# The last rows of a dense matrix in column halves, and its sum in two PSUM banks

## Chip, cores and metric

The kernel runs on one core of one Trainium2 chip. The metric is the device time of one execution in microseconds; lower is better.

## What is computed

A decode step for two sequences (B = 2, one token each, D = 448): the token's row is layer-normed, and the output is the row itself plus attention over the last 4,096 positions of a key and value cache plus a dense block with a Mish activation.

```python
xn = layernorm(x)                                   # 2 x 448
q = xn @ wq                                         # 448 x 4096: 16 heads of 256
s = q . k_cache[:, :, Sk - 4096:]  * 256 ** -0.5    # 8 kv heads, each for two query heads
o = softmax(s) . v_cache[:, :, Sk - 4096:]
A = o.reshape(2, 4096) @ wo                         # 4096 x 448
h = xn @ w1 + b1                                    # 448 x 1792
Bm = (h * tanh(softplus(h))) @ w2                   # 1792 x 448: the second dense matrix
out = x + A + Bm                                    # 2 x 448, bfloat16
```

All inputs are bfloat16. Keys and values of the window are 2 x 8 x 4,096 x 256 each, so 67 MB of the 78 MB that the kernel reads.

## The kernel before

The work goes in eight steps u = 0 to 7 of two kv heads each (`U = 8`, `KU = 2`). For each step the keys come in two loads of 4 MB (`load_k`), the values in two (`load_v`), and one load has the rows of `wo` that belong to its heads (`load_wo`). All of these loads, and those of `w1` and `w2`, are issued from SyncE's queue (SP) in the order in which the program names them. A load waits until its buffer is free: the big ones share a ring of three buffers (`ring`), which the keys, the values, `wq`, `w1` and `w2` take in turn. The schedule is written out by hand (`tc.manual_schedule()`): each engine runs its instructions in program order.

In a step VectorE transposes the keys in 32 x 32 blocks (`turns`, L271), TensorE makes the scores (`scores`, L347 and L358) into a PSUM tile `sc`, for which there are two buffers, ScalarE takes the exponential (L366), and VectorE turns the result into the layout that `values` needs (L369, L338 to L340). `values` (L404) multiplies it with the value rows, `weigh` makes the softmax denominators, `gather` and `finish` put the heads' outputs together and divide.

Steps 0 to 6 add their outputs times `wo` into the PSUM tile `early`. The last step does not: its value load is cut into pieces, so that the work behind the last value bytes is short, and its output goes through `mix` into a second sum, `acc`. That sum is laid out in four column groups of 112 (`G = 4`, `DG = 112`): group g lies on partitions 32g and 32g + 1, so the four groups of one product are four matmuls on four column blocks of TensorE. `carry` (L238, L240) copies `early` into `acc`'s groups, `add_rows` (L251) adds a product to all four.

The second dense matrix `w2` has 1,792 rows of 448. It is split in two halves k = 0 and 1 of 896 rows, and in each half partition p holds seven consecutive rows (`NI = 7`), 6,272 bytes that lie together in HBM. It is loaded last, behind the last values, in four parts (L556): (k, first row, last row + 1) of each partition are

```python
w2_parts = ((0, 0, NI), (1, 0, 4), (1, 4, 6), (1, 6, NI))
```

so 784, 448, 224 and 112 KB. `dense_out` takes the parts in the same order and makes one product for each row index i, four matmuls through `add_rows`. The activations `act_bf` that it multiplies are ready since the first step. At the end four copies move the groups of `acc` into the bfloat16 row `res`, groups 0 and 2 on VectorE (L621) and groups 1 and 3 on ScalarE (L623), and one store writes it (L624):

```python
for g in range(G):
    dst = res[:, g * DG : (g + 1) * DG]
    src = acc[32 * g : 32 * g + Bsz, :]
    if g % 2 == 0:
        nc.vector.tensor_copy(out=dst, in_=src)
    else:
        nc.scalar.copy(out=dst, in_=src)
nc.sync.dma_start(out=out.flatten_outer_dims(), in_=res[:])
```

The end of the program, in order: the loads of the last values, of the last `wo` rows and of the four parts of `w2`; `carry`; the last `values`, `weigh`, `gather`, `values_fixed` and `finish`; `mix`; the four `dense_out`; the copies and the store.

Of the kernel before, what the change touches and what calls it, by code (L numbers as in the profile page):

```python
# [12 lines left out]
FP32 = mybir.dt.float32  # L13
# [4 lines left out]
def kernel(  # L18
# [13 lines left out]
    nc = tc.nc  # L32
    P = 128
    G = 4
# [4 lines left out]
    Bsz, Sq, D = A_x.shape  # L39
# [22 lines left out]
    NI = F2 // P  # L62
    DG = D // G
# [14 lines left out]
    ps_sc = ctx.enter_context(tc.tile_pool(name="ps_sc", bufs=2, space=PSUM))  # L78
# [3 lines left out]
    ps_a = ctx.enter_context(tc.tile_pool(name="ps_a", bufs=1, space=PSUM))  # L82
# [7 lines left out]
    def ring(name):  # L90
        return kv_pool.tile([P, RK * KE], BF16, tag="kv", name=name)
# [18 lines left out]
    def load_wo(u):  # L110
# [22 lines left out]
        out=wq[:, 0 : NS * HW], in_=A_wq.flatten().rearrange("(p e) -> p e", p=P)  # L133
# [14 lines left out]
    for k in range(KU):  # L148
        nc.gpsimd.tensor_copy(
            out=hot[:, k, :, :, :, k],  # L150
            in_=ident[:].rearrange("p (q y) -> p y q", y=4).unsqueeze(2)
# [11 lines left out]
        out=rstd[:], in_=mv[:, 1:2], func=ACT.Sqrt, bias=eps_t[:], scale=1.0  # L163
# [4 lines left out]
        out=xn_bf[:],  # L168
# [8 lines left out]
        out=parm[:], in_=ident[:].rearrange("p (a o) -> p o a", o=2), axis=AXIS.X, op=ALU.add  # L177
# [3 lines left out]
        out=jm[:],  # L181
        in_=ident[:].rearrange("p (a j h) -> p j a h", j=J, h=rep),
# [4 lines left out]
        out=jm[:], in0=jm[:], scalar1=-1.0, scalar2=29952.0, op0=ALU.add, op1=ALU.mult  # L187
# [3 lines left out]
        out=mneg[:], in_=jm[:].unsqueeze(1).to_broadcast([P, TH * 8, J])  # L191
    )
    sel = consts.tile([P, 2, NQ], FP32)
    for x in range(2):
        for w in range(4):
            at = 32 * w + (2 * (w % 2) + x) * NQ
            src = ident[:, at : at + NQ]
            if w == 0:
                nc.vector.tensor_copy(out=sel[:, x, :], in_=src)
            else:  # L200
                nc.vector.tensor_tensor(
                    out=sel[:, x, :], in0=sel[:, x, :], in1=src, op=ALU.add
# [16 lines left out]
    for odd in range(2):  # L219
        for half in range(2):  # L220
            o = (half + odd) % 2
            nc.vector.tensor_scalar(
                out=xs[:, odd::2, half * Bsz : (half + 1) * Bsz],
# [7 lines left out]
    nc.tensor.matmul(  # L231
        early[:], lhsT=ident[0:Bsz, 0:Bsz], rhs=x_bf[:], start=True, stop=False
    )
    acc = ps_a.tile([P, DG], FP32)

    def carry():
        e_sb = small.tile([P, 2 * Dh], FP32, tag="vs", name="e_sb", bufs=1)[0:Bsz, 0:D]
        nc.scalar.copy(out=e_sb, in_=early[:])  # L238
        for g in range(G):
            nc.tensor.matmul(  # L240
                acc[32 * g : 32 * g + Bsz, :],
                lhsT=id2[:],
                rhs=e_sb[:, g * DG : (g + 1) * DG],
                start=True,
                stop=False,
                skip_group_check=True,
            )

    def add_rows(lhsT, rows, stop=False):
        for g in range(G):  # L250
            nc.tensor.matmul(  # L251
                acc[32 * g : 32 * g + Bsz, :],
                lhsT=lhsT,
                rhs=rows[:, g * DG : (g + 1) * DG],
                start=False,
                stop=stop,
                skip_group_check=True,
            )
# [20 lines left out]
    for n in range(2):  # L279
        for e in range(2):  # L280
# [3 lines left out]
                out=sp[:],  # L284
                in_=ident[:, o : o + 63 : 2].unsqueeze(1).to_broadcast([P, G, 32]),
# [91 lines left out]
    state = {}  # L377
# [113 lines left out]
    def mix(u):  # L491
        oT, w = state.pop(("oT", u)), wo_t.pop(u)
        for k2 in range(KU):
            for h in range(rep):
                for c in range(2):
                    add_rows(oT[:, c, k2 * rep + h, :], w[:, k2, h, c * D : (c + 1) * D])

    act_bf = consts.tile([P, NI, 2, Bsz], BF16)
# [46 lines left out]
        nc.vector.tensor_tensor(out=act_bf[:], in0=h_sb[:], in1=t_sb[:], op=ALU.mult)  # L545

    KH = 4096
    w2_parts = ((0, 0, NI), (1, 0, 4), (1, 4, 6), (1, 6, NI))

    def load_w2(part):  # L550
        if part == 0:
            state["w2"] = ring("w2")
        k, lo, hi = w2_parts[part]
        w2_in = B_w2.flatten().rearrange("(k p e) -> k p e", k=2, p=P)
        at = k * KH
        nc.sync.dma_start(  # L556
            out=state["w2"][:, at + lo * D : at + hi * D],
            in_=w2_in[k, :, lo * D : hi * D],
        )

    def dense_out(part):
        k, lo, hi = w2_parts[part]
        for i in range(lo, hi):
            at = k * KH + i * D
            add_rows(
                act_bf[:, i, k, :], state["w2"][:, at : at + D], stop=(k == 1 and i == NI - 1)
            )

    load_w1()
# [32 lines left out]
    for part in range(len(w2_parts)):  # L602
        load_w2(part)
    carry()
    values(u, 0)
    values(u, 1, 32)
# [6 lines left out]
    for part in range(len(w2_parts)):  # L613
        dense_out(part)

    res = consts.tile([Bsz, D], BF16)
    for g in range(G):
        dst = res[:, g * DG : (g + 1) * DG]
        src = acc[32 * g : 32 * g + Bsz, :]
        if g % 2 == 0:  # L620
            nc.vector.tensor_copy(out=dst, in_=src)  # L621
        else:
            nc.scalar.copy(out=dst, in_=src)  # L623
# [31 lines left out]
```

## Time and profile before

| | |
|---|---|
| median of 4 runs | 189.34 us (189.17 to 189.52) |
| the profiled execution's own time | 189.27 us |
| its span, first to last instruction | 187.5 us |
| busy: PE, PEld, DVE, ACT, POOL | 70.9, 33.1, 92.5, 12.5, 5.0 us |
| moved by DMA | 77.78 MB, mean 415 GB/s |
| DMA packets | 4,719, of which 740 under 512 B (485 of them semaphore writes of 4 B) |
| mean granted TensorE clock | 0.774 |

The profile is of one execution. Times in it are microseconds from the span's start. PE is TensorE's matmul, PEld its weight load, DVE VectorE, ACT ScalarE, SPq SyncE's DMA queue. A matmul's record ends where a model of its pipeline ends. "L251" is line 251 of the kernel, and a group of instructions is written with the tile that it writes, "<-", and the tiles that it reads. The chain of waits is followed back from the last instruction: each entry is the work, or the transfer, that released the next. For a DMA issue the page gives the KB and the time from issue to landing; a transfer is spread over 16 DMA engines, each of which reports its share by a semaphore event. A DMA engine's work is recorded packet by packet, a packet being one run of bytes.

### The profile page before, as it was taken

How to read it: one execution, taken by the hardware profiler on the slowest of the kernel's cores; microseconds unless marked ns; L12 is line 12 of the kernel's file. 1: busy time of each engine (PE TensorE's matmuls, PEld its weight loads, DVE VectorE, ACT ScalarE, POOL GpSimd, SP SyncE). 2: the span in 40 equal slices, each digit the busy share in tenths (PEclk: the TensorE clock that was granted, in tenths of full speed). 3: DMA queues.
4: the chain of work that ended last, by engine and by line, in shares of the span. 5: the costliest groups of instructions: out<-in, count | busy, mean ns of one | idle time of the engine just before them, and what ended most of it. 6: DMA issues, size and time to landing. Idle time of an engine off the chain costs nothing.

```text
span 187.5 us, 1938 instructions
## 1 busy us (share of the span) xinstructions
PE 70.9 (38%) x845; PEld 33.1 (18%) x849; DVE 92.5 (49%) x93; ACT 12.5 (7%) x26; POOL 5.0 (3%) x16
## 2 busy tenths in 40 slices
PE   0300277464109000882037002870065005854763
PEld 0100122431004000240012001430021002422452
DVE  5619714994892098028940395048910692040101
ACT  3000030101000100110001000110001000120101
POOL 8200000000000000000000000000000000000000
PEclk9999999999657955599558855698559755899655
DMA  6999999999999998999999999999999999999991
GB/s 224 441 421 398 441 426 422 473 444 426 419 413 426 444 449 378 482 440 447 399 447 409 433 440 412 455 447 437 426 406 440 419 440 426 440 406 405 434 405 50
DMA packets 4719, 77.78 MB, mean 415 GB/s; under 512 B 740, under 2 KB 1512, under 8 KB 2280
## 3 DMA queue, kind: packets, MB, share of 16 engines
q1 hardware_dynamic: 4436, 77.66, 96.8%
q8 instruction: 6, 0.10, 0.2%
q10 hardware_dynamic: 276, 0.01, 0.1%
q14 instruction: 1, 0.01, 0.0%
HBM read 77.67 MB, written 0.00 MB: 414 GB/s over the span
## 4 chain that ended last, share of the span: by engine, by line
DMA 59%; DVE 21%; PE 12%; issue 3%; ACT 2%; SPq 1%; another core or an unknown queue 1%; DVEq 0%
DMA v<-in_A_v_cache_dram 31%; DVE kt L271 16%; DMA k<-in_A_k_cache_dram 16%; DMA w<-in_B_w_dram 12%; PE pv L404 6%; PE sc L358 4%; DVE p L369 2%; PE o L422 1%; DVE rec L390 1%; ACT ex L366 1%; ACT vs L416 1%; PE acc L251 1%; DVE px L338 0%; DVE p L339 0%
## 5 line engine op out<-in xcount | busy, mean ns | idle before, releaser
L271 DVE STREAM_TRANSPOSE kt<-k 128x4096 f32<-128x4096 f32 x16 | 70.0, 4414 | 36.7 <-DMA k<-in_A_k_cache_dram 36.7
L404 PE MATMUL pv<-v,p 128*32 128x512 bf16 x240 | 23.6, 562 | 74.7 <-DMA v<-in_A_v_cache_dram 74.7
L404 PEld LDWEIGHTS <-p 128*32 128x32 bf16 x240 | 8.8, 130 | 87.4 <-issue 64.4
L358 PE MATMUL sc<-kt,qd 128*32 128x512 bf16 x256 | 19.3, 440 | 3.1 <-DVE qd L326 1.4
L449 DVE TENSOR_TENSOR oT<-o,rec 128x16 bf16<-128x16 f32 x4 | 0.7, 175 | 23.8 <-PE o L422 19.0
L369 DVE STREAM_TRANSPOSE p<-ex 128x512 bf16<-128x512 bf16 x8 | 5.2, 690 | 10.2 <-ACT ex L366 10.2
L366 ACT ACTIVATE ex<-sc 128x512 bf16<-128x512 f32 x8 | 4.8, 597 | 72.8 <-PE sc L358 72.8
L358 PEld LDWEIGHTS <-qd 128*32 128x32 bf16 x256 | 6.8, 103 | 12.7 <-issue 6.8
L293 PE MATMUL q_ps<-wq,xs 128*32 128x512 bf16 x28 | 3.2, 628 | 14.0 <-DMA wq<-in_A_wq_dram 14.0
L390 DVE TENSOR_REDUCE rec<-dn 128x8 f32<-128x512 f32 x4 | 2.8, 692 | 10.4 <-PE dn L382 9.0
L416 ACT COPY vs<-pv 128x512 f32<-128x512 f32 x4 | 2.3, 586 | 57.8 <-PE pv L404 57.8
L422 PE MATMUL o<-sel,vs 128*128 128x8 f32 x32 | 5.2, 289 | 2.1 <-ACT vs L416 2.1
L422 PEld LDWEIGHTS o<-sel,vs 128*128 128x128 f32 x32 | 4.8, 228 | 5.5 <-ACT vs L416 5.5
L483 PE MATMUL early<-wo,ox 128*2 128x448 bf16 x24 | 5.0, 352 | 1.9 <-ACT ox L474 1.9
L293 PEld LDWEIGHTS <-xs 128*32 128x32 bf16 x28 | 1.1, 136 | 15.6 <-issue 15.6
L513 PE MATMUL h_ps<-xs,w 128*128 128x4 bf16 x49 | 2.8, 193 | 2.5 <-DMA w<-in_B_w_dram 2.5
L382 PE MATMUL dn<-p,ones 128*128 128x512 bf16 x5 | 2.0, 433 | 4.1 <-DVE p L340 3.8
L214 PE MATMUL xr_ps<-ident,xrows 2*128 2x2 bf16 x7 | 1.0, 181 | 6.7 <-DVE xrows L213 6.7
L513 PEld LDWEIGHTS <-w 128*128 128x128 bf16 x49 | 2.7, 152 | 3.4 <-DMA w<-in_B_w_dram 3.4
L347 PE MATMUL sc<-mneg,ident 128*128 128x512 bf16 x7 | 2.9, 412 | 0.0
L437 PE MATMUL o<-p,v 128*128 128x8 bf16 x64 | 1.9, 168 | 2.2 <-DMA v<-in_A_v_cache_dram 2.2
L310 DVE COPY qT<-qt_ps 128x16 bf16<-128x16 bf16 x4 | 0.4, 168 | 4.4 <-PE qt_ps L305 4.4
(65 smaller groups left out, 40.8 us busy)
## 6 DMA issues: line engine op xcount, KB each, us to landing
k<-in_A_k_cache_dram SPq DMA_DIRECT2D x8, 4096.0 KB, 27.4
v<-in_A_v_cache_dram SPq DMA_DIRECT2D x7, 4096.0 KB, 21.1
wq<-in_A_wq_dram SPq DMA_DIRECT2D x1, 3584.0 KB, 20.6
wo<-in_A_wo_dram SPq DMA_DIRECT2D x3, 896.0 KB, 20.5
v<-in_A_v_cache_dram SPq DMA_DIRECT2D x1, 2048.0 KB, 17.6
w<-in_B_w_dram SPq DMA_DIRECT2D x1, 1568.0 KB, 13.1
v<-in_A_v_cache_dram SPq DMA_DIRECT2D x1, 1536.0 KB, 21.7
wo<-in_A_wo_dram SPq DMA_DIRECT2D x2, 448.0 KB
```

Source lines behind the costliest of these rows:

```text
L271: nc.vector.transpose(out=kt[i][:, :, r, :, :], in_=t[:, r * KE : (r + 1) * KE].bitcast(FP32).rearrange("p (a c j) -> p a c j", c=P // (R ...
L293: nc.tensor.matmul(q_ps[32 * u : 32 * (u + 1), :], lhsT=xs[:, s, :], rhs=wq_t[s][:, u * 512 : (u + 1) * 512], start=(s == 0), stop=(s == N ...
L347: nc.tensor.matmul(sc[:].rearrange("p t c m -> p (t c m)"), lhsT=ident[:], rhs=mneg[:].rearrange("p a j -> p (a j)"), start=True, stop=Fal ...
L358: nc.tensor.matmul(sc[32 * w : 32 * (w + 1)].rearrange("p t c m -> p t (c m)"), lhsT=qd[:, u, 2 * n + e, :, :].rearrange("p g q -> p (g q) ...
L366: nc.scalar.activation(out=ex[:, :, :, i, :], in_=sc[:], func=ACT.Exp, scale=scale)
L369: nc.vector.transpose(out=p_all[:, :, h * TH : (h + 1) * TH, :].rearrange("p g t q -> p t g q"), in_=ex[:, h * TH : (h + 1) * TH].rearrang ...
L390: nc.vector.tensor_reduce(out=rec[:], in_=dn[:].rearrange("p a q -> p q a"), axis=AXIS.X, op=ALU.add)
L404: nc.tensor.matmul(pv[32 * w : 32 * (w + 1), :, :].rearrange("p x d -> p (x d)"), lhsT=p_run[:, g, 4 * a : 4 * a + 4, :].rearrange("p t q ...
L416: nc.scalar.copy(out=sb[:].rearrange("p x d -> p (x d)"), in_=pv[:].rearrange("p x d -> p (x d)"))
L422: nc.tensor.matmul(po[:, c, :], lhsT=sb[:, x, c::2], rhs=sel[:, x, :], start=(x == 0 and c == 0), stop=(last and x == 1), skip_group_check ...
L483: nc.tensor.matmul(early[:], lhsT=ox[:, i, :], rhs=w[:, i, :], start=False, stop=(u == U - 2 and i == 7),)
L513: nc.tensor.matmul(h_ps[:, i, :, :].rearrange("p k b -> p (k b)"), lhsT=w1_v[:, s, i, :], rhs=xs[:, s, 0 : 2 * Bsz], start=(s == 0), stop= ...
```

## The change

The sum lies in two PSUM tiles: the left half of the columns (groups 0 and 1) in `acc`'s own bank, the right half (groups 2 and 3) in a buffer of the scores' tile `sc`. The partitions of the groups stay. The second half of `w2` comes in other parts: five rows of each partition whole (560 KB), then the left column half of the last two rows, then their right half (112 KB each). Half a row is 224 elements, 448 bytes; the two half rows of a partition are two such runs. `add_rows` takes the groups that it is to add to, and `dense_out` gives it those of the part. The order of the copies in the program and their engines stay.

```diff
-    acc = ps_a.tile([P, DG], FP32)
+    acc = []
+
+    def acc_at(g):
+        return acc[g // 2][32 * g : 32 * g + Bsz, 0:DG]
 
     def carry():
+        acc.append(ps_a.tile([P, DG], FP32, name="acc"))
+        acc.append(ps_sc.tile([P, 4 * P], FP32, tag="sc", name="acc2"))
         e_sb = small.tile([P, 2 * Dh], FP32, tag="vs", name="e_sb", bufs=1)[0:Bsz, 0:D]
         nc.scalar.copy(out=e_sb, in_=early[:])
         for g in range(G):
             nc.tensor.matmul(
-                acc[32 * g : 32 * g + Bsz, :],
+                acc_at(g),
...
-    def add_rows(lhsT, rows, stop=False):
-        for g in range(G):
+    def add_rows(lhsT, rows, stop=False, groups=range(G)):
+        for g in groups:
             nc.tensor.matmul(
-                acc[32 * g : 32 * g + Bsz, :],
+                acc_at(g),
                 lhsT=lhsT,
-                rhs=rows[:, g * DG : (g + 1) * DG],
+                rhs=rows[:, (g - groups[0]) * DG : (g - groups[0] + 1) * DG],
...
-    w2_parts = ((0, 0, NI), (1, 0, 4), (1, 4, 6), (1, 6, NI))
+    w2_parts = ((0, 0, NI, 0, G), (1, 0, 5, 0, G), (1, 5, NI, 0, 2), (1, 5, NI, 2, G))
 
     def load_w2(part):
         if part == 0:
             state["w2"] = ring("w2")
-        k, lo, hi = w2_parts[part]
-        w2_in = B_w2.flatten().rearrange("(k p e) -> k p e", k=2, p=P)
-        at = k * KH
-        nc.sync.dma_start(
-            out=state["w2"][:, at + lo * D : at + hi * D],
-            in_=w2_in[k, :, lo * D : hi * D],
-        )
+        k, lo, hi, g0, g1 = w2_parts[part]
+        w2_in = B_w2.rearrange("(k p i) d -> k p i d", k=2, p=P)
+        nc.sync.dma_start(out=w2_rows(part), in_=w2_in[k, :, lo:hi, g0 * DG : g1 * DG])
+
+    def w2_rows(part):
+        k, lo, hi, g0, g1 = w2_parts[part]
+        at = k * KH + lo * D if g1 - g0 == G else 2 * KH + g0 * 2 * P
+        wide = (g1 - g0) * DG
+        return state["w2"][:, at : at + (hi - lo) * wide].rearrange("p (i d) -> p i d", d=wide)
 
     def dense_out(part):
-        k, lo, hi = w2_parts[part]
+        k, lo, hi, g0, g1 = w2_parts[part]
+        rows = w2_rows(part)
         for i in range(lo, hi):
-            at = k * KH + i * D
             add_rows(
-                act_bf[:, i, k, :], state["w2"][:, at : at + D], stop=(k == 1 and i == NI - 1)
+                act_bf[:, i, k, :],
+                rows[:, i - lo, :],
+                stop=(k == 1 and i == NI - 1),
+                groups=range(g0, g1),
             )
...
-        src = acc[32 * g : 32 * g + Bsz, :]
+        src = acc_at(g)
```

## The prediction

> **What bounds the kernel now.** I read the page's slices and queue rows first, then the last part of the chain of waits, the timeline of the last four microseconds, the rows of the DMA issues, and the busy times by stage. The slices and queues:
>
> ```profile
> DMA  6999999999999998999999999999999999999991
> ...
> q1 hardware_dynamic: 4436, 77.66, 96.8%
> q8 instruction: 6, 0.10, 0.2%
> ```
>
> The DMA engines are full from the second slice to the last but one, and one queue, SP's, has nearly all of it. So the kernel ends when the last byte has landed, plus what must still be done with it. The end of the chain (start, length, what):
>
> ```profile
> 160.98 22.73 DMA w<-in_B_w_dram
> 183.71 0.04 issue
> 183.75 1.12 PE acc L251 x25
> 184.87 0.25 DVE res L621
> 185.13 0.30 DVEq L650
> ```
>
> The chain hangs on the second dense matrix, then on 1.1 us of short matmuls, then on the copies of the sum. The timeline of that stretch:
>
> ```profile
> 183.75 1.08 PE L251 MATMUL acc<-w,act_bf 128*2 128x112 bf16 x28 [0.26 <-DMA w<-in_B_w_dram]
> 184.86 0.56 DVE L621 CAST res<-acc 2x112 bf16<-2x112 f32 x2 [3.30 <-PE acc L251]
> 184.90 0.51 ACT L623 CAST res<-acc 2x112 bf16<-2x112 f32 x2 [9.56 <-PE acc L251]
> 185.49 0.32 SPq L624 DMA_DIRECT2D out_dram<-res  x1
> ```
>
> These 28 matmuls are three bursts, one for each landing. The trace's semaphore events put the landings of the last three parts at 183.71, 184.24 and 184.53; the bursts begin 0.04 later each. VectorE and ScalarE make two copies each, one after the other, and only then the store goes out. So the tail behind the last landing L = 184.53 is: matmuls from L+0.04, four completion signals at L+0.31 to L+0.41, the first pair of copies from L+0.33, the second pair until L+0.91, the store at L+0.96. The span ends 1.99 later, at 187.48. The parts' issues:
>
> ```profile
> w<-in_B_w_dram SPq DMA_DIRECT2D x1, 784.0 KB, 22.1
> w<-in_B_w_dram SPq DMA_DIRECT2D x1, 448.0 KB, 22.7
> w<-in_B_w_dram SPq DMA_DIRECT2D x1, 224.0 KB, 15.4
> w<-in_B_w_dram SPq DMA_DIRECT2D x1, 112.0 KB, 11.0
> ```
>
> They were issued 11 to 23 us ahead of their landings: the queue is never empty, and when a part lands is set by the packets ahead of it on each engine. By stage (length, busy time of PE, PEld, DVE, ACT, POOL, granted clock, DMA share, GB/s):
>
> ```profile
> 178.00:182.00 4.00, 2.25 (x84) 2.17 (x88) 0.17 (x1) 0.00 (x0) 0.00 (x0) 0.50 1.02 420
> 182.00:184.00 2.00, 1.60 (x68) 1.24 (x57) 0.00 (x0) 0.00 (x0) 0.00 (x0) 0.50 0.66 248
> ```
>
> In the last 2 us the share falls to 0.66: the semaphore events of the 112 KB part spread from 182.90 to 184.53, eleven engines by 183.95 and five after 184.43. Each engine works its own list back to back, so the five late ones decide, and every nanosecond that the change adds to an engine's list moves the end.
>
> **Part by part.** *The packets.* The trace records each packet's size and duration: 896 B 41 ns, 1,792 B 74, 3,584 B 140, 4,096 B 159, 6,272 B 239, and on an engine the next begins 3.4 ns before the end of the last. So a packet steps by 37.6, 70.7, 136.5 or 235.6 ns, which is 4.5 ns and 0.0369 ns a byte. An engine serves 8 of the 128 partitions. For the matrix's second half its list was 8 packets of 3,584, 8 of 1,792 and 8 of 896 B: 8 x (136.5 + 70.7 + 37.6) = 1,958 ns. The change makes it 8 of 4,480 B (five rows that lie together, 4.5 + 165.2 = 169.7 ns each) and 32 of 448 B, since half a row does not touch the next half row in HBM. No row shows a 448 B packet. On the line it steps by 4.5 + 16.5 = 21.0 ns: 1,358 + 672 = 2,030 ns, **0.07 us later**. The lower bound is bytes without the 4.5: 16.5 ns, 1,886 in all, 0.07 earlier. The upper bound is that it steps no faster than the 896 B packet, 37.6 ns: 2,561 in all, 0.60 later. I take the line, because short packets lie on it too: the bias's 14 B packets took 9 ns and the semaphore writes of 4 B 9 ns, where the line gives 8.4 and 8.0. Both are far from twice that, but they are far from 448 B as well, so I keep the ends.
>
> The Trainium skill, "DMA: Bandwidth & Descriptors", Specifications, speaks against this edit: it gives 512 B as the smallest transfer at line rate and says that below it the engine reads, modifies and writes. The 14 B rows show no such cost in the engine's record. If the rule held as a second pass over the bytes, my estimate from that page would be 37.5 ns a packet and a kernel 0.4 us slower, where the line gives 0.1 us faster.
>
> *The copies.* The left half (groups 0 and 1) is complete when the third part lands, 16 packets or 0.34 us before the last. Its four matmuls stand two deep in a column group, as the eight of the 224 KB part did: that burst began at 184.28 and signalled at 184.66, 0.38 later. So the left copies run from about L-0.34+0.04+0.38+0.02 = L+0.10 and end, at 0.28 a copy with its signal (184.86 to 185.14), by L+0.38. The right half's signals come at L+0.04+0.38 = L+0.42 and its copies start at L+0.44. So the left pair is hidden, with 0.06 to spare. If that cover went, the second copy would wait again, at most the whole 0.28. One pair then stands in the tail: L+0.44+0.28 = L+0.72, the store 0.05 later at L+0.77, where it was at L+0.96. **Gain 0.19 us**; with the four signals' spacing of 0.03 counted either way, 0.15 to 0.23.
>
> *TensorE.* There are 56 matmuls before and after. The last part has four in both, now two deep (counted above). The second part has 20 instead of 16; at the 0.019 us a matmul of the first burst (28 starts from 182.67 to 183.20) its last starts 0.38 after the burst's first at L-0.64, at L-0.26, while the left half is ready at L-0.30: 0.04 lost of the 0.06 that covers the left copies, nothing for the right half, which starts at L+0.04.
>
> *SP's queue.* The matrix's parts are still four issues behind the same waits. The last two carry 8 more packets per engine each. The issue rows of 448 and 224 KB lasted 6.6 and 1.9 us, so room in the queue runs out at times; the last was issued at 173.57 and its first packet moved at 182.27. The 16 KB packets ahead, 0.61 us each, had all landed by 173.56; 16 more entries of then 0.07 us are 1.1 us, against 8.7 of lead. Behind them SP has only the store. Nothing.
>
> *The second bank.* It is the score buffer whose last reader, an exponential (L366), is long done when the first sums are made at 167.65. No wait. The sums of the four groups go to four quadrants as before, and the first copy already started at 184.86, before the fourth signal at 184.94. Nothing.
>
> **Sum.** -0.19 + 0.07 = -0.12 us. The profiled execution took 189.27 (span 187.48 and 1.79 around it), 0.07 below the median of 189.34. Against the median: **189.22 us**.
>
> **Rivals.** *Slower: the half rows cost as whole rows.* The place is each late engine's last 32 packets, the price 0.60 us as bounded above. With a step of x ns the list is 32x - 600 ns longer; the gain of 0.19 is eaten at x = 24.7, and at x = 36.6 the kernel is 0.2% slower. At 37.6: -0.19 + 0.60 = +0.41, **189.75**; at twice the line (42 ns) 189.89. For it: no row between 14 and 896 B. Against it: the straight line on both sides.
>
> *The rows that lie together are not joined.* The new access pattern names rows and columns apart. If each row became a packet, the first half's list goes from 8 x 235.6 = 1,885 to 56 x 37.6 = 2,106 ns, and the five rows from 1,358 to 40 x 37.6 = 1,504: 0.37 more, +0.25 in all, **189.59**. Against it: nothing in the memory order forbids joining.
>
> *The left copies are not hidden.* Cover is thin (0.02 to 0.06). With all four copies behind the last signal the change costs its packets alone: +0.07, **189.41**. That is also what comes if the edit doesn't do what it says.
>
> *Faster by more.* Packets at the lower bound and a whole pair of copies gone (185.14 to 185.44, 0.30): -0.37, **188.97**.
>
> *An instruction fetch moves.* The q8 row is six packets of 16 KB that each hold up one engine by over a microsecond: the spread of landings within a part grows from 0.7 to 1.8 us after the first, at 39 us. Five of them made the five late engines. Two on one engine would add some 1.2 us, **190.4**. Against it: the number of instructions stays.
>
> **How the numbers follow.** The sum 0.52 (own range 189.1 to 189.4); whole-row cost 0.29; rows not joined 0.05; copies not hidden 0.06; faster by more 0.05; a fetch 0.03. The range is 189.0 to 189.85: it takes in the whole-row case at 189.75, and leaves out the fetch, half of the faster case and packets dearer still. A measurement of this kernel can tell about 0.2%, 0.38 us, from no change. Slower by that: four fifths of the whole-row case, the fetch, and a part of the unjoined rows, 0.28. Faster: half of the fast case and the low tail of the sum, 0.06. Within: 0.66.
>
> **What would show it.** Right: packets under 512 B go from 740 to 1,252, each half-row packet at about 25 ns; the last landing is near 184.60, the DVE copy in two rows with the first ended before the last matmuls signal, the store 0.77 behind the last landing. Wrong: half-row packets at 40 ns or more, with the last landing at 185.1; first-half packets of 896 B; both copies back to back; or an engine with two fetches.

## The result

The changed kernel takes 189.71 us (median of 40 runs, 189.55 to 189.95) where the kernel before took 189.46 (60 runs, 189.17 to 189.68): a ratio of 1.0015, with a 95% interval of 1.0010 to 1.0019. It is 0.25 us slower. The prediction was 0.12 us faster, so the time fell into the range but the change went the other way. The difference lies inside the 0.2% that the prediction called no change; it could be told from zero only over that many runs.

The page of the changed kernel, its packet row:

```profile
DMA packets 4975, 77.78 MB, mean 414 GB/s; under 512 B 1252, under 2 KB 1768, under 8 KB 2536
```

The 512 half-row packets are there (1,252 under 512 B, 740 before), and no first-half row became a packet of its own. The end of the chain of waits (start, length, what):

```profile
161.04 23.00 DMA w<-in_B_w_dram
184.04 0.04 issue
184.08 0.86 PE acc L256 x21
184.94 0.25 DVE res L631
185.20 0.31 DVEq L660
185.51 0.02 issue
185.53 0.25 ACT res L633
```

A member is new at the end: behind VectorE's copies the chain goes on through a copy of ScalarE. The timeline of that stretch, with what ended the idle time of each in brackets:

```profile
184.08 1.02 PE L256 MATMUL acc<-w,act_bf 128*2 128x112 bf16 x28 [0.54 <-DMA w<-in_B_w_dram]
184.93 0.56 DVE L631 CAST res<-acc 2x112 bf16<-2x112 f32 x2 [3.30 <-PE acc L256]
184.97 0.24 ACT L633 CAST res<-acc 2x112 bf16<-2x112 f32 x1 [9.53 <-PE acc L256]
185.53 0.25 ACT L633 CAST res<-acc 2x112 bf16<-2x112 f32 x1 [0.32 <-DVE res L631]
185.80 0.34 SPq L634 DMA_DIRECT2D out_dram<-res  x1
```

Before, ScalarE's two copies stood in one row of two, 0.51 us long, beside VectorE's. Now the second one starts 0.56 after the first, and its bracket names VectorE: it waited 0.32 us for VectorE's copy of the *other* group. The list of waits has the same as a row that was not there before:

```profile
ACT res L633 <- DVE res L631: 0.3, 1, 0.3
```

In single rows, each copy with its completion signal: the left half landed at 184.39 and the right half at 184.71 (the last landing, L). VectorE's copies ran from 184.93 to 185.21 and from 185.23 to 185.51, ScalarE's from 184.97 to 185.22 and from 185.53 to 185.79. The store went out at 185.80, L+1.09. It was L+0.96 before and should have been L+0.77.

For most runs below I use two lengths of the profiled execution, one profile for each kernel. The *list* is the time from the landing of the first half of `w2` to the last landing: what the late DMA engines need for the second half. The *tail* is from there to the store's issue. The last landing itself lies anywhere from 184.53 to 184.99 in the profiles of the six kernels that have the parts of before; their lists lie between 1.90 and 1.93. List and tail are 1.904 and 0.958 before and 2.033 and 1.090 after, together 0.26 more. The measured 0.25 is all there.

| kernel | list | tail | both, against before | ratio of times (95%) |
|---|---|---|---|---|
| before | 1.904 | 0.958 | | |
| the change | 2.033 | 1.090 | +0.26 | 1.0015 (1.0010 to 1.0019) |
| two banks, wide | 1.910 | 1.200 | +0.25 | 1.0011 (1.0002 to 1.0019) |
| two banks, narrow | 1.924 | 0.956 | +0.02 | 0.9996 (0.9987 to 1.0005) |
| one bank, wide | 1.921 | 1.497 | +0.56 | 1.0031 (1.0019 to 1.0043) |
| change, narrow | 2.012 | 0.867 | +0.02 | 1.0003 (0.9994 to 1.0011) |
| change, one bank | 2.013 | 0.864 | +0.02 | 0.9997 (0.9988 to 1.0006) |
| five parts | 2.057 | 0.758 | -0.05 | 1.0004 (0.9995 to 1.0013) |

### The profile page after: what moved, and what is told of

Read it like the earlier page. It is cut to its first block, busy times and chain, and to the rows that moved or that the text cites. A ratio compares the mean times of both kernels' runs of the same rounds, so it can differ in the third digit from the quotient of the medians.

```text
span 187.8 us, 1938 instructions
## 1 busy us (share of the span) xinstructions
PE 71.3 (38%) x845; PEld 33.1 (18%) x849; DVE 92.5 (49%) x93; ACT 12.5 (7%) x26; POOL 5.0 (3%) x16
## 2 busy tenths in 40 slices
DMA packets 4975, 77.78 MB, mean 414 GB/s; under 512 B 1252, under 2 KB 1768, under 8 KB 2536
## 4 chain that ended last, share of the span: by engine, by line
DMA 59%; DVE 21%; PE 12%; issue 3%; ACT 2%; SPq 1%; another core or an unknown queue 1%; DVEq 0%
DMA v<-in_A_v_cache_dram 31%; DVE kt L276 16%; DMA k<-in_A_k_cache_dram 16%; DMA w<-in_B_w_dram 12%; PE pv L409 6%; PE sc L363 4%; DVE p L374 2%; PE o L427 1%; DVE rec L395 1%; ACT ex L371 1%; ACT vs L421 1%; PE dn L387 1%; DVE px L343 0%; DVE p L344 0%
```

## Experiments: where the wait comes from

No kernel here names a wait. The layer that turns the program into instructions writes the semaphores, from which tiles each instruction reads and writes. The second sum had been allocated 512 columns wide, of which 112 are used. My theory (W) was that this width brought the wait; the rival (P), that the 448 B packets had eaten the time and the wait stood beside something else.

**Two banks alone (banks_wide).** The parts of `w2` stay as before:

```diff
+        acc.append(ps_a.tile([P, DG], FP32, name="acc"))
+        acc.append(ps_sc.tile([P, 4 * P], FP32, tag="sc", name="acc2"))
```

> The kernel before with the two banks of the change and nothing else of it: parts and copies as before, the second sum in a PSUM tile of 512 columns. Theory W (the loss is a wait that came in with the wide second sum: ScalarE's last copy waits for VectorE's last copy): that copy starts after VectorE's second one has ended, 0.3 us later than before, the store 0.30 later; landings unchanged; ratio to before about 1.0015. Rival P (the loss is all in the 448 B packets): no difference, 1.0000.

Its timeline at the end:

```profile
185.32 0.56 DVE L626 CAST res<-acc 2x112 bf16<-2x112 f32 x2 [3.28 <-PE acc L256]
185.35 0.24 ACT L628 CAST res<-acc 2x112 bf16<-2x112 f32 x1 [9.46 <-PE acc L256]
185.91 0.25 ACT L628 CAST res<-acc 2x112 bf16<-2x112 f32 x1 [0.32 <-DVE res L626]
186.19 0.32 SPq L629 DMA_DIRECT2D out_dram<-res  x1
```

Without a single half-row packet the wait of 0.32 is there, the tail is 0.24 longer, and the ratio is 1.0011. The list is as before. P can't make this.

**The same, 112 columns wide (banks_narrow).**

```diff
-        acc.append(ps_sc.tile([P, 4 * P], FP32, tag="sc", name="acc2"))
+        acc.append(ps_sc.tile([P, DG], FP32, tag="sc", name="acc2"))
```

> As the kernel with two banks alone, but the second sum's tile is 112 columns wide, as the first is, in the same buffer. Theory W: the wait is gone, ScalarE's two copies run back to back beside VectorE's, ratio 1.0000 to before. If the second bank itself costs something: still 1.0015.

```profile
184.92 0.56 DVE L626 CAST res<-acc 2x112 bf16<-2x112 f32 x2 [3.29 <-PE acc L256]
184.96 0.51 ACT L628 CAST res<-acc 2x112 bf16<-2x112 f32 x2 [9.54 <-PE acc L256]
185.55 0.34 SPq L629 DMA_DIRECT2D out_dram<-res  x1
```

Same buffer, same bank, and ScalarE's copies are again one row of two; tail 0.956, no difference in time. So neither the second bank nor the scores' buffer costs anything that can be measured here.

**One bank, only wider (one_bank_wide).** The kernel before, with one sum:

```diff
-    acc = ps_a.tile([P, DG], FP32)
+    acc = ps_a.tile([P, 4 * P], FP32)
```

and `0:DG` where it is used.

> The kernel before, with nothing changed but the width of its one sum's PSUM tile: 512 columns, of which the first 112 are used as before. Theory W': it is the tile's unused width that brings the wait, not the second bank; then all four copies wait for each other and run one by one, 0.28 to 0.30 each, the first 0.08 later than before because it waits for the last matmul: store at 1.47 to 1.55 behind the last landing instead of 0.96, ratio 1.0027 to 1.0031. Rival: the wait belongs to the second bank or to the scores' buffer: no difference.

```profile
185.03 0.26 DVE L621 CAST res<-acc 2x112 bf16<-2x112 f32 x1 [3.31 <-PE acc L251]
185.32 0.24 ACT L623 CAST res<-acc 2x112 bf16<-2x112 f32 x1 [9.48 <-DVE res L621]
185.60 0.27 DVE L621 CAST res<-acc 2x112 bf16<-2x112 f32 x1 [0.31 <-ACT res L623]
185.90 0.25 ACT L623 CAST res<-acc 2x112 bf16<-2x112 f32 x1 [0.33 <-DVE res L621]
186.17 0.33 SPq L624 DMA_DIRECT2D out_dram<-res  x1
```

This settles it. One number in an allocation (the `0:DG` keeps the columns in use the same), and the four copies wait for each other in turn, from the second on each bracket naming the other engine: 0.54 us of tail, ratio 1.0031. The trace also has one completion signal for the last four matmuls (at 185.00, 0.33 behind the last landing) where the kernel before has four (0.31 to 0.41 behind it); it comes so early that the first copy starts only 0.02 later than before, not the 0.08 expected. What is shown is that the allocated width does it, 512 columns against 112 with the same columns in use. No width in between was tried, so it stays open whether any unused column is enough, and what rule in the layer does it.

## Experiments: what the rest of the change does

**The change without the wait (halves_narrow)**: the one-line edit of the narrow tile, on the changed kernel.

> The whole change, with the second sum's tile 112 columns wide instead of 512. Theory W: ScalarE's last copy starts with the right half's signal (about 0.42 behind the last landing) and VectorE's last copy, which ends 0.79 behind it, sets the store at 0.85, 0.24 earlier than in the changed kernel; 0.11 of tail gained on before against some 0.10 of packets: ratio to before 0.9995 to 1.0005. Rival P: as the changed kernel, 1.0015.

```profile
184.05 1.00 PE L256 MATMUL acc<-w,act_bf 128*2 128x112 bf16 x28 [0.54 <-DMA w<-in_B_w_dram]
184.90 0.56 DVE L631 CAST res<-acc 2x112 bf16<-2x112 f32 x2 [3.33 <-PE acc L256]
184.93 0.51 ACT L633 CAST res<-acc 2x112 bf16<-2x112 f32 x2 [9.36 <-PE acc L256]
185.53 0.32 SPq L634 DMA_DIRECT2D out_dram<-res  x1
```

The tail falls from 1.090 to 0.867, and the ratio to before is 1.0003. The wait was worth 0.22 us. What is left, 0.09 of tail gained against 0.11 of list lost, can't be told from nothing.

**The halves in one bank (halves_one_bank)**: `acc.append(acc[0])` in place of the second tile, so that all groups are on their own partitions of one bank.

> The whole change in parts and order, but all four groups stay in one bank, as before. If the second bank is needed to copy the left half while the right one is summed: the left copies start only behind the right half's matmuls, all four copies in the tail, ratio 1.0005. If different partitions of one bank are enough (as the first copy of before already began ahead of the last signal): as the change with the narrow second sum, 0.9995 to 1.0005.

Tail 0.864, as with two banks: VectorE's left copy started at 0.24 behind the last landing in both, while the matmuls of the right half were still going:

```profile
184.31 1.00 PE L256 MATMUL acc<-w,act_bf 128*2 128x112 bf16 x28 [0.54 <-DMA w<-in_B_w_dram]
185.16 0.56 DVE L631 CAST res<-acc 2x112 bf16<-2x112 f32 x2 [3.34 <-PE acc L256]
```

The second bank was not needed to copy one half while the other is summed. The Trainium skill, "PSUM — Partial Sum Buffer", Terms, says so in its entry on the quadrant: different groups of 32 partitions of one bank may be accessed at the same time. This run agrees.

**Less work ahead of the left half (five_parts)**: the narrow tile, and the 560 KB part cut in two.

```diff
-    w2_parts = ((0, 0, NI, 0, G), (1, 0, 5, 0, G), (1, 5, NI, 0, 2), (1, 5, NI, 2, G))
+    w2_parts = ((0, 0, NI, 0, G), (1, 0, 3, 0, G), (1, 3, 5, 0, G),
+                (1, 5, NI, 0, 2), (1, 5, NI, 2, G))
```

> The change with the second sum 112 columns wide, and the 560 KB part cut in two (rows 0 to 2, then 3 and 4), so that only 8 matmuls stand ahead of the left half's. Theory C (in the change the left copies came late because 20 matmuls stood between the part before and the left half; the left pair then pushed VectorE's right copy by 0.08): the left copies end before the right half's signals, both right copies start at about 0.44 behind the last landing, store at 0.77 to 0.79 instead of 0.87; ratio to before 0.999 to 1.000. Rival (the left half's matmuls are slow in themselves, as they go two deep in half the column groups): left copies still start 0.2 behind the last landing, store at 0.87.

```profile
184.73 0.60 DVE L631 CAST res<-acc 2x112 bf16<-2x112 f32 x2 [3.21 <-PE acc L256]
184.77 0.58 ACT L633 CAST res<-acc 2x112 bf16<-2x112 f32 x2 [9.23 <-PE acc L256]
185.40 0.32 SPq L634 DMA_DIRECT2D out_dram<-res  x1
```

Here the two copies of each engine no longer touch: 0.60 in a row where two copies back to back take 0.56. The left ones end at 185.01 and the right ones start with their own signals at 185.07 and 185.10. The tail is 0.758, which is the 0.77 of the prediction. The fifth part makes the list 0.02 to 0.04 longer still, and the whole, 0.05 us better by the two lengths, doesn't show in the time (1.0004, 0.9995 to 1.0013). It is the best version of this idea that I found, and it does not beat the kernel before by anything that can be measured.

**The price of short packets (packets_896, packets_448).** All four parts of the kernel before in runs of 896 or 448 B, otherwise the same:

```diff
             in_=w2_in[k, :, lo * D : hi * D],
+            max_dma_last_dim=448,
```

> As the kernel with all of the second matrix in runs of 448 B, but 896 B: 112 packets on each engine at 37.6 ns, 4.21 us instead of 3.84: 0.37 us slower, ratio 1.0019. A cost that sets in only under 512 B would show as a 448 B kernel much more than 2.5 times as far from before as this one.

> The kernel before, with all four parts of the second matrix moved in runs of 448 B (224 of them on each DMA engine, instead of 32 longer ones). If a 448 B packet steps by 21.0 to 21.5 ns as on the line: the lists of the two halves take 4.70 to 4.82 us instead of 3.84, so 0.86 to 1.0 us slower, ratio 1.0045 to 1.0053. If such a packet passes the engine twice (37.5 ns): 8.4 us, 4.6 us slower, ratio 1.024.

The packet row of the second:

```profile
DMA packets 7791, 77.78 MB, mean 411 GB/s; under 512 B 4324, under 2 KB 4840, under 8 KB 5352
```

With 896 B the way from the landing of the last values to the last landing was 4.168 us instead of 3.853: 0.32 more (0.37 expected), ratio 1.0018 (1.0009 to 1.0027). With 448 B it was 5.246, 1.39 more, ratio 1.0068 (1.0054 to 1.0082); 0.22 of that comes from a sixth engine, which the landings show behind the late five after the instruction fetch at 182.99 (1.19 us long). On the other five it is 1.17, which makes some 22.4 ns for each of the 224 packets (5.02 us in all): above the line's 21.0, and far below 37.5. Up to 181.5 us every record of a 448 B packet is 25 ns long, as predicted, and the next one mostly begins 21 or 22 ns after it. From 181.5 to 183.5 us, 228 of 1,359 records are over 30 ns long; I did not find the cause. The way from before to 448 B is 3.7 times as far as that from before to 896 B (1.17 against 0.32), where the line has 2.3 to 2.6, so there is some extra cost, but no second pass over the bytes. The Trainium skill, "DMA: Bandwidth & Descriptors", Specifications, says that below 512 B an engine reads, modifies and writes; nothing in the time of these loads from HBM to SBUF shows it.

**Another way to save the second round of copies (one_copy, one_copy_one_store).** Not part of the change, but the same 0.3 us. One VectorE instruction copies all groups at once, partition by partition, and the stores gather them:

```diff
-    res = consts.tile([Bsz, D], BF16)
-    for g in range(G):
...
+    res = consts.tile([P, DG], BF16)
+    nc.vector.tensor_copy(out=res[:], in_=acc[:])
+    nc.sync.dma_start(out=rows[0], in_=res[0::32, :])
+    nc.scalar.dma_start(out=rows[1], in_=res[1::32, :])
```

> The kernel before with its parts, but another end: the first sums write all 32 rows of each group, one VectorE copy takes all 128 partitions of the sum, and two stores of four rows, one from SP's queue and one from ScalarE's, write the two output rows. If what the tail costs is the second round of copies: the copy starts at 0.43 behind the last landing, ends at 0.71, stores at 0.76 instead of 0.96; 0.2 us faster, ratio 0.9985 to 0.9995. Rival: the two stores of 224 B rows land later than the one did, or the second queue's issue comes late, and take the gain back: ratio 1.000 or over.

```profile
185.06 0.28 DVE L617 CAST res<-acc 128x112 bf16<-128x112 f32 x1 [3.36 <-PE acc L251]
185.37 0.66 SPq L619 DMA_DIRECT2D out_dram<-res  x1
185.37 0.58 ACTq L620 DMA_DIRECT2D out_dram<-res  x1
```

The copy did its part: stores at 0.66 behind the last landing instead of 0.96. But their issues lasted 0.66 and 0.58 us instead of 0.32, and the later one landed 1.98 after it was issued, where the one store of before took 1.16. Ratio 1.0036 (1.0023 to 1.0049). The rival that the expectation names, a later landing, had it. With the batch rows 16 partitions apart, one store is enough:

> As the kernel with one copy and two stores, but one store: the two batch rows of a group stand 16 partitions apart, so that eight partitions at equal steps hold the output and one DMA from SP's queue writes them. The last step's output and the activations lie in rows of 48 columns, of which each matmul takes 32 as weights; the other rows of the sum hold values that are not stored. Copy ends 0.64 behind the last landing and the store goes out at 0.66 instead of 0.96. If one store of eight 224 B rows takes as long as the one of two 896 B rows (1.16 from issue to landing): 0.3 us faster, ratio 0.9984. If it takes as long as the slower of the two stores before (1.98): 0.5 us slower, 1.0027. In between, break even at 1.46.

```profile
185.03 0.27 DVE L630 CAST res<-acc 128x112 bf16<-128x112 f32 x1 [3.33 <-PE acc L256]
185.33 0.68 SPq L631 DMA_DIRECT2D out_dram<-res  x1
```

Issued at 0.68, landed 1.70 later: 0.54 more than before against 0.28 gained. Ratio 1.0018 (1.0010 to 1.0027). The wide form of the store costs more than the copies that it saves.

## Why the prediction was wrong, step by step

The prediction had -0.19 for the copies and +0.07 for the packets. The copies came to +0.13 (tail 1.090 against 0.958). The packets came to +0.11: the list is 2.019 in the mean of the three kernels with the change's parts, and 1.913 in that of the six with the parts of before, the two with one copy among them. The 0.36 between -0.12 and +0.24 divides into three terms.

- **"The second bank. ... No wait. ... Nothing": this is the step that failed.** It checked that the buffer was free and that the partitions differed, which were right (banks_narrow, halves_one_bank). It did not ask what the layer that writes the waits makes of a sum in a tile four and a half times as wide as the part in use. The new wait between the two copies costs 0.22 us (1.090 against 0.867). That alone turns the sign. The diff shows the width, `[P, 4 * P]` beside `[P, DG]`, and the trace of before could not price it. The bound from both sides that such an edit needs would have been the 0.30 of one more copy in the tail. None of the rivals was this; the nearest, that the left copies are not hidden, has the same look of copies one behind the other, but the left pair was hidden here and the right pair was not side by side.
- **"The left pair is hidden, with 0.06 to spare" was off by 0.14.** The left half's first matmul started 0.12 after its landing and not 0.04, because the 20 matmuls of the part before were still going, five rows deep at 0.093 us a row where the prediction took 0.076 (four times 0.019); and two matmuls deep in two column groups signalled 0.41 and 0.44 after the start of the first, where I had taken 0.38. The left copies ended at L+0.49, and VectorE's right copy, forecast for L+0.44, started at L+0.52 (L+0.53 with the narrow tile). That is the 0.10 between 0.867 and 0.77, and five_parts got it back. The prediction had already given 0.04 of those 0.06 to the backlog. The 0.02 left was less than its sizes were sure to, and it still counted the pair as hidden.
- **The packets were 0.11 and not 0.07.** The new packets were as forecast: five rows in steps of 169.4 ns, all 512 half rows in records of 25 ns, the next one mostly 21 or 22 ns after, and the list with them 2.019 where the sum was 2.030. What was off is the list of before: the sum made it 1.958, and it measures 1.913 (1.904 in the profile that the prediction was made from). Why it is shorter than its sum is not shown. The whole-row rival (0.60) is ruled out by the packet records and by packets_448.

Right were the packet count, the joined rows, the part that SP's queue does not play, and that the instruction fetches stay (six, as before). The size of the tail was right too, had the change come without its wait and its backlog: 0.758 (five_parts) against 0.77. The time of 189.22 that the prediction named lies 0.49 below the 189.71 measured: 0.37 is the change, and 0.12 is that the kernel before has a median of 189.46 over 60 runs, not the 189.34 of the first four.

## What to carry to other kernels

When a change moves a tile to another allocation, look at its shape as well as its place: here 400 unused columns made two engines take turns, for 0.22 us at the one point where nothing hides it. Read the brackets of the last instructions: an engine waiting for another engine's *read* is a wait that no data asks for. And when a kernel ends behind a full DMA queue, write its last few microseconds as two lengths, list and tail: here they were steady (lists within 0.02) where the landings were not.

## What the runs showed of the hardware

- The store's form mattered more than its bytes, which are the same 1,792 in all three: two rows of 896 B landed 1.16 us after issue, eight of 224 B 1.70, and two stores of four rows each, from two queues at once, 1.62 and 1.98.
- One instruction copying 128 partitions of 112 columns took 0.275 us, one copying two partitions 0.264: the partitions are all but free.
- An instruction fetch of 16 KB that hits a DMA engine while it works its last short packets can make it the last one (packets_448: 0.22 us behind the others, one fetch at 182.99).
